# Gate and up stage: where the loads, sums and stores of the blocks without a partner stand

## The chip, the cores and the metric

The kernel runs on one core of a Trainium2 chip. The metric is the device time of one execution in microseconds (us). Five engines work side by side, each in its own order, and wait for one another through semaphores: TensorE (PE; its weight loads are listed as PEld), VectorE (DVE), ScalarE (ACT), GpSimd (POOL) and SyncE (SP). In this kernel SyncE and GpSimd do little but issue DMAs; a DMA whose buffer or data is not ready holds up the ones behind it in its queue.

## The reference

One input x of 2048 positions by 640 features goes through two branches, and a gate per position mixes them.

```python
def _A_ref(x, dft_seq_re, dft_seq_im, dft_hid_re, dft_hid_im):
    a = jnp.einsum("bsd,ed->bse", x, dft_hid_re)
    b = jnp.einsum("bsd,ed->bse", x, dft_hid_im)
    y = jnp.einsum("ts,bse->bte", dft_seq_re, a) - jnp.einsum("ts,bse->bte", dft_seq_im, b)
    return y

def _B_ref(x, w_gate, w_up, w_down):
    return (_gelu(x @ w_gate) * (x @ w_up)) @ w_down

x = A_x
g = _sigmoid((x * gate_w).sum(-1, keepdims=True))
a = _A_ref(x, A_dft_seq_re, A_dft_seq_im, A_dft_hid_re, A_dft_hid_im)
b = _B_ref(x, B_w_gate, B_w_up, B_w_down)
return g * a + (1 - g) * b
```

The hidden width of the second branch is 1728, that is 13 blocks of 128 and one of 64. All values are 32-bit floats.

## The kernel before

**Products.** Every operand of a product is split into a high part in the matrix format (written by ScalarE, helper `high`, L80) and a low part, the rest (written by VectorE, helper `low`, L83). `mm3` then issues three matmuls for one product, high by high, high by low and low by high (L99, L100, L101). On top of that the large products are done in the manner of Strassen: of a two by two product of blocks only seven block products are computed, from sums of the operands, so weights, inputs and hidden values are all needed as sums too. VectorE makes these sums.

**Stages.** The gate and up stage comes first and computes the hidden values, block after block of the hidden width. The down stage follows, then the two DFT products. Hidden values are stored to DRAM as they are made, with their sums (`hA`, `hT`, by `keep`, L390, on GpSimd's queue), and are read again in the down stage, which starts after some 300 us.

**Blocks.** Block 0 and the narrow block of 64 are computed before the loop; the loop at L1174 runs blocks f = 1 to 12. `pair_of(f)` gives a block's kind: 0 for blocks 1 and 2, then 1 for the odd blocks and 2 for the even ones from 3 on (an odd and the next even block share some products, `together` and `together_up`). `gate_up` (L487) is the work of one block on one half of the positions (tp = 0 and 1), in steps that the loop takes turns with: a matmul group, then what ScalarE or VectorE does with its bank. Three places matter here. In L537 VectorE adds bank X to `s5`; in L546 TensorE then adds the product of the u5 weights to the same bank X, so it has to wait until both halves' L537 have read; in L541 and L542 the other half of the block's result is summed and sent through gelu.

**Fills.** What VectorE and ScalarE must do for the next block (splits and sums of its weights, `make_w`; wa, wb, wq and ws are such weight tiles, ra, rb and rq their raw loads) stands in a list, `fills`, of pairs of a cost and a piece of work. `fill` (L1150) issues pieces between the steps, as many as are due: the costs done so far are held to 1.25 times the share of the block's matmul work that is issued. What is left in the list is issued at the block's end.

```python
while fills and not (some and not fills[0][0]) and state["done"] <= 1.25 * state["all"] * state["pe"] / state["pe_all"]:
    cost, do = fills.popleft()
```

**The blocks without a partner.** The hidden width has 14 blocks; the down stage pairs blocks 1 to 12 and is left with block 0 and the narrow block. Their hidden values (`h0`) and down weights (`wd0`, `wdr`) need sums of their own. `LEFT_AT` (L677) gives these to five blocks of the gate and up stage: to blocks 2 and 8 `sum_h0` (three loads, three sums, four stores to `hL`; tiles lf), to blocks 6 and 10 `sum_h0_narrow` (six loads, three sums, one store; tiles lg), to block 4 `sum_left` (five loads, six sums, two stores to `wsl`; tiles lw, lm, ld, ls). Each of these functions issues its loads at once, on SyncE's queue, and returns the sums as pieces for `fills`; a piece issues its stores behind its sums, on SyncE's queue as well. The loop calls the function at the block's start and puts the sums into the middle of `fills`, ahead of the second half of the next block's weight work. Only the down stage reads `hL` and `wsl`.

**Order and buffers.** TensorE, ScalarE, VectorE and GpSimd keep the written order here (`in_order`, L1173). SyncE's DMAs are not in that list: the recording layer lets one go ahead as soon as its tile has a buffer, so their order in the queue can differ from the written one. The tiles of 128 by 512 (`mtile`, L73: the lf, lg, lw tiles, the s tiles of `gate_up`, the xp and xv tiles of sums over positions, loaded for block 3's shared products) share 14 buffers; one that a store reads is free once the store has landed. SyncE's queue also carries the next blocks' weights (`load_w(f + 2)` in step 5 of a block, L1244; `load_up` and `sum_wd`, tiles wu, dr and da, at the start of an odd block) and the tiles xz of the gate's sum over features (L726, L730). GpSimd's queue carries `keep` and loads of sums over positions (xq and xu, L1145).

Of the kernel before, what the change touches and what calls it, by code (L numbers as in the profile page):

```python
# [23 lines left out]
FR = F - NF * P  # L24
# [11 lines left out]
def kernel(  # L36
# [27 lines left out]
    nc = tc.nc  # L64
# [5 lines left out]
    def slot(dt, shape, name):  # L70
        return pool.tile(shape, dt, tag="s4", name=name, bufs=46)

    def mtile(dt, name):  # L73
        return pool.tile([P, T], dt, tag="m", name=name, bufs=14)
# [30 lines left out]
    @contextmanager  # L105
    def in_order(*engines):

        traced = nc.cur_bb.bb.instructions
        mark = traced[-1]
        yield  # L110
        start = next(k for k in reversed(range(len(traced))) if traced[k] is mark) + 1
        dep = mybir.DependencyInfo(mybir.DependencyClass.NoSync, mybir.DependencyReason.DATA)
        prev = {}
        for ins in traced[start:]:
            if ins.engine in engines:
                if ins.engine in prev:
                    tc.add_manual_dep(ins, prev[ins.engine].name, dep, reason="in_order")
                prev[ins.engine] = ins
# [10 lines left out]
    wsl = dram.tile([P, 8, P], F32, tag="wsl", name="wsl")  # L129
    hL = [dram.tile([P, 4, T], F32, tag=f"hL{p}", name=f"hL{p}") for p in range(2)]  # L130
# [476 lines left out]
    def chunks(name):  # L607
        return mtile(F32, name).rearrange("p (b c) -> p b c", c=P)

    def sum_left():  # L610


        w, m, d = chunks("lw"), chunks("lm"), chunks("ld")
        nc.sync.dma_start(w, wd0[:, :4])
        for q in range(2):
            rows = slice(q * FR, (q + 1) * FR)
            nc.sync.dma_start(m[rows], wdr[:, :4])
            nc.sync.dma_start(d[rows], wd0[:FR, :4])
        a11, a21, a22 = w[:, 0:2], w[:, 2:4], m[:, 2:4]
        own = {}  # L620

        def first():
            s = own["s"] = chunks("ls")
            tt(s[:, 0:2], a21, a11, op=ALU.subtract)
            tt(a21[:FR], a21[:FR], a22[:FR], op=ALU.add)
            tt(m[:, 0:2], m[:, 0:2], a22, op=ALU.subtract)

        def second():
            s = own["s"]
            tt(a11, a11, a21, op=ALU.subtract)  # L630
            tt(d[:, 0:2], d[:, 0:2], d[:, 2:4], op=ALU.subtract)
            tt(s[:, 2:4], m[:, 0:2], d[:, 0:2], op=ALU.add)
            nc.sync.dma_start(wsl[:, 0:4], w)
            nc.sync.dma_start(wsl[:, 4:8], s)

        return [(100, first), (100, second)]

    def sum_h0(tp):


        f1, f2, b22 = (mtile(F32, f"lf{tp}{k}") for k in range(3))
        for v, k in ((f1, 0), (f2, 1), (b22, 3)):
            nc.sync.dma_start(v, h0[tp][:, k])

        def first():
            tt(f1, f2, f1, op=ALU.subtract)
            for k in (0, 2):
                rows = slice(FR if k else 0, P)
                nc.sync.dma_start(hL[tp][rows, k], f1[rows])
            tt(f2[:FR], f2[:FR], b22[:FR], op=ALU.subtract)  # L650
            nc.sync.dma_start(hL[tp][:, 3], f2)
            tt(b22[:FR], f1[:FR], b22[:FR], op=ALU.subtract)
            nc.sync.dma_start(hL[tp][:FR, 2], b22[:FR])

        return [(183, first)]

    def sum_h0_narrow(tp):


        d1, d2, b21, b22 = (mtile(F32, f"lg{tp}{k}") for k in range(4))  # L660
        for v, k in ((d1, 0), (d2, 1)):
            for q in range(2):
                nc.sync.dma_start(v[q * FR : (q + 1) * FR], h0[tp][:FR, k])
        for v, k in ((b21, 2), (b22, 3)):
            nc.sync.dma_start(v, h0[tp][:, k])

        def first():
            tt(d2, d2, d1, op=ALU.subtract)
            tt(b21, b21, b22, op=ALU.subtract)

        def second():
            tt(b21, b21, d2, op=ALU.add)
            nc.sync.dma_start(hL[tp][:, 1], b21)

        return [(122, first), (61, second)]

    LEFT_AT = {2: partial(sum_h0, 0), 4: sum_left, 6: partial(sum_h0_narrow, 0), 8: partial(sum_h0, 1), 10: partial(sum_h0_narrow, 1)}  # L677

# [464 lines left out]
    def load_across(f, n, to, kept, k):  # L1143
        v = slot(F32R, [P, 2, T], f"{n}{f}{k}")
        nc.gpsimd.dma_start(v.bitcast(F32), kept[k - 1])  # L1145
        to[f"T{k}"] = v[:, 0], v[:, 1]

    fills, state = deque(), {}
# [24 lines left out]
    with in_order(PE, ACT, DVE, POOL):  # L1173
        for f in range(1, NF):  # L1174
            kind = pair_of(f)
            if f == PAIRED:
                loadu()
                fills.extend([*t4, *u123[:3], *late_work, *u123[3:], *u4])
            fills.extend(todo)
            todo.clear()  # L1180
            if kind == 1:
                up, work = make_up(f, load_up(f))
                fills.extend(work)
            if kind == 1:
                lw, *w = sum_wd((f - PAIRED) // 2)
                lw[1]()
                fills.extend(w)
            if f == PAIRED - 1:
                loadp()
                fills.extend(t123)  # L1190
            if f == NF - 1:
                lw, *w = sum_wd(NK - 1)
                lw[1]()
                fills.extend(w)
            if f + 1 < NF:
                nxt, work = make_w(f + 1)
                if kind != 1 or f == PAIRED:
                    fills.extend(work)
            if kind == 1 and f > PAIRED:
                (_, first), z1, (_, second), z2 = load_z(2)  # L1200
                first()
                k = len(fills) // 2
                more = list(fills)
                fills.clear()
                fills.extend([*more[:k], z1, (0, second), *more[k:], z2, *work])
            elif f in ZE_AT:
                (_, first), z1 = load_z(1)
                first()
                fills.insert(5, z1)
            if f in LEFT_AT:  # L1210
                more = LEFT_AT[f]()
                k = len(fills) // 2
                rest = [fills.pop() for _ in range(len(fills) - k)]
                fills.extend([*more, *reversed(rest)])
            if f == NF - 1:
                load_k(0)
                fills.extend(split_pieces(0))
                gates(0)
                nc.scalar.activation(table, table, AF.Gelu_apprx_tanh)
            state.update(pe=0, done=0, all=sum(c for c, _ in fills), pe_all=2450 if not kind else 2994 if kind == 1 else 1768)  # L1220
            s5 = pair(F32, f"s5{f}")
            xs = {}
            work = [gate_up(f, W, Bs[tp], tp, s5[:, tp], s1t, xs, s4) for tp in range(2)]
            more = together(f, W, Tp, s1t, xs) if kind == 1 else iter(())
            more_up = together_up(f, W, up, s4) if kind == 1 else iter(())
            for _ in range(4):
                run(more)
            for step in range(8 if not kind else 7):
                for tp, w in enumerate(work):
                    run(w)  # L1230
                    if (step, tp) in ((0, 1), (1, 1)):
                        run(more)
                        if step == 0:
                            run(more)
                    if (2, 0) < (step, tp) < (6, 0):
                        run(more_up)
                if step < 2 and kind == 1 and f > PAIRED:
                    for k in ((1,), (2, 3))[step]:
                        load_across(f, "xu", Tu, keptu, k)
                if step == 4 and pair_of(f + 1) == 1 and f + 1 > PAIRED:  # L1240
                    for k in (1, 2, 3):
                        load_across(f + 1, "xq", Tp, keptp, k)
                if step == 5:
                    load_w(f + 2)  # L1244
                if f == NF - 1 and step > 4:
                    load_k(step - 4)
            for v in (more, more_up):
                next(v, None)
            while fills:
                fills.popleft()[1]()  # L1250
            W = nxt
# [80 lines left out]
    for i, (j, ri, b, sp) in enumerate(cseq):  # L1332
# [21 lines left out]
        if not b:  # L1354
# [17 lines left out]
            if lst:  # L1372
# [4 lines left out]
                for d in range(2):  # L1377
                    c = sv["c11", d]
# [83 lines left out]
    for i, (tp, b, p) in enumerate(useq[: 3 * ND]):  # L1462
# [22 lines left out]
        if not b:  # L1485
            for q in range(2):
                sv["c11", q] = copy(X[q], f"ys{n}{q}")
            for q in range(2):
                c = sv["c11", q]
# [76 lines left out]
    for ps, w, b, t in ((Z, "S4", 3, 1), (V, "A12", 2, 0)):  # L1566
        which = ends[2 - 2 * t : 4 - 2 * t]
        gated_high(which)
        for q in range(2):
# [3 lines left out]
            v = es[q][0] if t else sv["x", q]  # L1573
# [20 lines left out]
    for ps, cols in zip(parts_of, halves):  # L1594
# [3 lines left out]
        v = vs[1][:, cols]  # L1598
# [68 lines left out]
```

## Time and profile before

| | |
|---|---|
| runs of the kernel before | 1023.54, 1027.96, 1030.12 us (median 1027.96) |
| profiled execution | 1022.09 us, of which the span from first to last instruction is 1020.3 us |
| granted TensorE clock | 1.000 |
| DMA traffic | 269.15 MB, mean 264 GB/s |
| gate and up stage, blocks 2 to 10 | about 72 to 287 us |

A block of kind 0 lasts some 23 us in this profile, an odd block from 3 on 30 us, an even one 18 us. In a row of the timeline the columns are the start in us, the duration, engine, line and operation, what is written from what, and in brackets the engine's idle time just before and what ended it. A row of the waits gives the engine and tile that waited, what it waited for, and total, number and longest in us. Matmuls overlap: a row's duration reaches into the next matmul, so their rate is read from their starts.

### The profile page before, as it was taken

The page shows a single profiled execution, that of the slowest core. Times are in us where ns is not written, and L with a number is a line of the kernel's source. Part 1 is how long each engine was busy: PE and PEld are TensorE (multiplying, and loading weights), DVE is VectorE, ACT ScalarE, POOL GpSimd, SP SyncE. Part 2 cuts the span into 40 slices and gives each one's busy share as a digit, 9 for nine tenths or more (in the row PEclk, how much of TensorE's full clock was granted, in tenths as well). Part 3 has the DMA queues.
Part 4 walks back from the last instruction along what each step waited for, and adds up shares of the span by engine and source line. Part 5 has one row for each costly group of instructions (what it writes and reads, how often), then busy time and mean ns, then how long its engine had stood idle before and what let it go on. Part 6 is the DMA issues. An engine that isn't in the chain of part 4 may idle for free.

```text
span 1020.3 us, 13287 instructions
## 1 busy us (share of the span) xinstructions
PE 1015.7 (100%) x4483; PEld 839.3 (82%) x4483; DVE 824.0 (81%) x1163; ACT 486.0 (48%) x635; POOL 166.9 (16%) x295
## 2 busy tenths in 40 slices
PE   9999999999999999999999999999999999999998
PEld 7888878888888888888888888888888888888887
DVE  6977877787877979988898975897588859797796
ACT  5544534353635577466455343444344445455440
POOL 0122232323231200100011022102210200021112
PEclk9999999999999999999999999999999999999999
DMA  7456598979798999969766778658866877997856
GB/s 270 168 187 237 195 292 282 304 250 336 231 320 297 403 331 373 346 258 355 258 236 192 246 269 305 217 193 288 307 205 209 293 255 269 326 321 217 262 149 97
DMA packets 98084, 269.15 MB, mean 264 GB/s; under 512 B 12832, under 2 KB 28064, under 8 KB 98016
## 3 DMA queue, kind: packets, MB, share of 16 engines
q1 hardware_dynamic: 72096, 186.94, 53.1%
q0 software_dynamic: 25776, 81.30, 24.2%
q8 instruction: 35, 0.57, 0.2%
q14 instruction: 33, 0.27, 0.1%
q10 hardware_dynamic: 144, 0.07, 0.0%
HBM read 193.53 MB, written 70.80 MB: 259 GB/s over the span
## 4 chain that ended last, share of the span: by engine, by line
PE 88%; issue 8%; POOL 2%; DVE 1%; DMA 1%; POOLq 0%; DVEq 0%
PE pX L100 5%; PE pX L99 5%; PE pX L101 5%; PE pZ L100 4%; PE pZ L99 4%; PE pZ L101 4%; PE pL L99 3%; PE pL L100 3%; PE pL L101 3%; PE pY L99 1%; PE pQ L99 1%; PE pR L99 1%; PE pV L99 1%; PE pV L100 1%; PE pR L101 1%
## 5 line engine op out<-in xcount | busy, mean ns | idle before, releaser
L80 ACT ACTIVATE ch<-csa 128x1024 fp32r<-128x1024 f32 x32 | 34.0, 1063 | 89.4 <-DVE csa L777 70.6
L83 DVE TENSOR_TENSOR cl<-cra,ch 128x1024 fp32r<-128x1024 f32 x32 | 39.1, 1222 | 23.5 <-ACT ch L80 23.3
L80 ACT ACTIVATE ch<-cra 128x1024 fp32r<-128x1024 f32 x32 | 33.9, 1059 | 47.5 <-PE pL L100 15.3
L83 DVE TENSOR_TENSOR cl<-crb,ch 128x1024 fp32r<-128x1024 f32 x32 | 39.1, 1221 | 15.5 <-ACT ch L80 15.4
L101 PE MATMUL pL<-ch,xal 128*128 128x512 f32 x128 | 49.8, 389 | 0.0
L100 PE MATMUL pL<-cl,xah 128*128 128x512 f32 x128 | 49.8, 389 | 0.0
L99 PE MATMUL pL<-ch,xah 128*128 128x512 f32 x128 | 49.3, 389 | 0.0
L390 POOL DMA_DIRECT2D hA<-s x48 | 26.1, 544 | 126.7 <-DVE s L548 107.2
L80 ACT ACTIVATE ch<-crb 128x1024 fp32r<-128x1024 f32 x32 | 33.8, 1055 | 25.8 <-DVE cl L83 12.4
L83 DVE TENSOR_TENSOR cl<-csb,ch 128x1024 fp32r<-128x1024 f32 x32 | 39.1, 1223 | 4.3 <-ACT ch L80 2.3
L83 DVE TENSOR_TENSOR cl<-csa,ch 128x1024 fp32r<-128x1024 f32 x32 | 39.1, 1222 | 2.9 <-PE pR L100 1.7
L80 ACT ACTIVATE ch<-csb 128x1024 fp32r<-128x1024 f32 x32 | 34.0, 1062 | 12.5 <-PE pR L101 4.5
L83 DVE TENSOR_TENSOR kl<-kw,kh 128x1024 fp32r<-128x1024 f32 x26 | 31.7, 1220 | 6.5 <-ACT kh L80 6.5
L542 ACT ACTIVATE s<-s 128x512 f32<-128x512 f32 x24 | 15.2, 633 | 45.2 <-DVE s L541 45.2
L1328 POOL DMA_DIRECT2D uA<-c x8 | 4.3, 541 | 169.8 <-DVE c L1416 169.6
L914 POOL DMA_DIRECT2D out<-ks x12 | 6.5, 542 | 153.8 <-DVE ks L913 153.1
L390 POOL DMA_DIRECT2D hT<-s x48 | 26.0, 541 | 26.9 <-DVE s L565 9.3
L147 ACT ACTIVATE s<-pX 128x512 f32<-128x512 f32 x40 | 23.1, 596 | 14.8 <-PE pX L101 14.3
L80 ACT ACTIVATE kh<-kw 128x1024 fp32r<-128x1024 f32 x26 | 27.2, 1048 | 2.1 <-DMA kw<-wsd 2.1
L101 PEld LDWEIGHTS pL<-ch,xal 128*128 128x128 f32 x128 | 24.0, 188 | 5.0
L99 PEld LDWEIGHTS pL<-ch,xah 128*128 128x128 f32 x128 | 24.0, 188 | 5.0
L100 PEld LDWEIGHTS pL<-cl,xah 128*128 128x128 f32 x128 | 24.0, 188 | 5.0
(3612 smaller groups left out, 3467.9 us busy)
## 6 DMA issues: line engine op xcount, KB each, us to landing
cra<-in_ct SPq DMA_DIRECT2D x64, 512.0 KB, 4.0
crb<-in_ct SPq DMA_DIRECT2D x64, 512.0 KB, 5.2
hA<-s POOLq DMA_DIRECT2D x48, 256.0 KB, 4.5
hT<-s POOLq DMA_DIRECT2D x48, 256.0 KB, 5.7
kr<-hA SPq DMA_DIRECT2D x24, 512.0 KB, 7.3
kr<-hT SPq DMA_DIRECT2D x24, 512.0 KB, 7.5
ux<-uA SPq DMA_DIRECT2D x24, 512.0 KB, 6.1
ux<-uT SPq DMA_DIRECT2D x16, 512.0 KB, 5.8
```

The source lines that it names most:

```text
L80: nc.scalar.activation(hi, raw, AF.Copy)
L83: nc.vector.tensor_tensor(lo, raw, hi.bitcast(F32), op=ALU.subtract)
L99: nc.tensor.matmul(ps, lh, rh, start=first, stop=False, skip_group_check=True)
L100: nc.tensor.matmul(ps, lh, rl, start=False, stop=False, skip_group_check=True)
L101: nc.tensor.matmul(ps, ll, rh, start=False, stop=last, skip_group_check=True)
L147: nc.scalar.activation(m, src, AF.Copy)
L390: nc.gpsimd.dma_start(to[:, i], src)
L542: nc.scalar.activation(s2, s2, AF.Gelu_apprx_tanh)
L914: nc.gpsimd.dma_start(acc4[:, t] if tp and e == 4 else out[2 * tp + t, e], src)
L1328: nc.gpsimd.dma_start(to[:, i], src)
```

## The change

The five functions keep their loads and sums. Their stores are no longer issued behind the sums but gathered in a list, `left_out`, which the loop issues when the next block begins. The loop calls the function after step 3 of the block instead of at its start, and appends the sums to the end of `fills`, adding their costs to the block's total then.

```diff
         def second():
             ...
-            nc.sync.dma_start(wsl[:, 0:4], w)
-            nc.sync.dma_start(wsl[:, 4:8], s)
+            left_out.append((wsl[:, 0:4], w))
+            left_out.append((wsl[:, 4:8], s))
 ...
             for k in (0, 2):
                 rows = slice(FR if k else 0, P)
-                nc.sync.dma_start(hL[tp][rows, k], f1[rows])
+                left_out.append((hL[tp][rows, k], f1[rows]))
 ...
             tt(b21, b21, d2, op=ALU.add)
-            nc.sync.dma_start(hL[tp][:, 1], b21)
+            left_out.append((hL[tp][:, 1], b21))
 ...
+    left_out = []
 ...
             if f == PAIRED:
                 loadu()
                 fills.extend([*t4, *u123[:3], *late_work, *u123[3:], *u4])
+            for to, v in left_out:
+                nc.sync.dma_start(to, v)
+            left_out.clear()
             fills.extend(todo)
 ...
-            if f in LEFT_AT:
-                more = LEFT_AT[f]()
-                k = len(fills) // 2
-                rest = [fills.pop() for _ in range(len(fills) - k)]
-                fills.extend([*more, *reversed(rest)])
 ...
+                if step == 3 and f in LEFT_AT:
+                    left = LEFT_AT[f]()
+                    fills.extend(left)
+                    state["all"] += sum(c for c, _ in left)
                 if step == 5:
                     load_w(f + 2)
```

The two other stores of `sum_h0` are changed in the same way.

More of the change, by code (lines that the diff above doesn't have):

```diff
@@ L648, in first @@
                 rows = slice(FR if k else 0, P)
-                nc.sync.dma_start(hL[tp][rows, k], f1[rows])
+                left_out.append((hL[tp][rows, k], f1[rows]))
             tt(f2[:FR], f2[:FR], b22[:FR], op=ALU.subtract)
-            nc.sync.dma_start(hL[tp][:, 3], f2)
+            left_out.append((hL[tp][:, 3], f2))
             tt(b22[:FR], f1[:FR], b22[:FR], op=ALU.subtract)
-            nc.sync.dma_start(hL[tp][:FR, 2], b22[:FR])
+            left_out.append((hL[tp][:FR, 2], b22[:FR]))
         return [(183, first)]
```

## The prediction

> **What bounds the kernel now.** I read the page first, then the waits of TensorE, then the gate and up stage alone.
>
> ```profile
> span 1020.3 us, 13287 instructions
> PE 1015.7 (100%) x4483; PEld 839.3 (82%) x4483; DVE 824.0 (81%) x1163; ACT 486.0 (48%) x635; POOL 166.9 (16%) x295
> ...
> PE idle L1015 <- PEq L1655: 0.8, 1, 0.8
> PE pH5t L99 <- DMA xq<-xp: 0.3, 1, 0.3
> ```
>
> The last two rows are all the waits that TensorE has in the whole span: 0.8 us at the start and 0.3 us before one matmul of block 5. A busy share of 100% could still hide slow matmuls, so I look at their spacing, in the block where the change puts most instructions, and at the window around it.
>
> ```profile
> 125.00:143.00 18.00, 18.00 (x81) 14.93 (x80) 14.99 (x33) 9.43 (x15) 6.66 (x11) 1.00 0.81 228
> ...
> 141.45 0.39 PE L99 MATMUL pX<-x05h,wa 128*128 128x512 f32 x1
> ...
> 142.13 0.39 PE L99 MATMUL pX<-x15h,wa 128*128 128x512 f32 x1
> ...
> L100 PEld LDWEIGHTS pX<-x011l,wa 128*128 128x128 f32 x2 | 0.4, 188 | 0.1
> ```
>
> The first row is the table by stretches (stretch, length, busy time of TensorE, its weight loads, VectorE, ScalarE and GpSimd, then the granted clock, the DMA share and GB/s), the next two are from the timeline, the last groups weight loads by form. Three products lie between the two matmuls shown, so starts are 0.68 / 3 = 0.227 us apart, at a granted clock of 1.00. 4483 matmuls at 0.227 us are about 1016 us of the 1020.3 us span. So everything that is not a matmul following a matmul is worth about 4 us, 0.4%, and the change touches no matmul. That is the ceiling of any gain. What the change can do is turn VectorE's or SyncE's order into a new wait of TensorE; the working below asks how much slack each moved step has.
>
> The Trainium skill (Perfetto Trace Analysis, Identifying the Most-Contended Engine) speaks against this reading: it calls TensorE's matmul busy share a poor measure of headroom and prefers the share of weight loads, here 82%, by which some 18% of the span, an estimate of 184 us, would be open. In this trace it is not: each load takes 188 ns of a 227 ns spacing, 83%, so the loads' share is what back-to-back matmuls give.
>
> **The change part by part.** Work is neither added nor removed: the same 18 sums, 23 loads and 12 stores. The build keeps TensorE's order the same. VectorE's order changes in blocks 2, 4, 6, 8 and 10 alone: the sums go from ahead of the next block's weight sums (ws) to behind the last weight split (ws low), next to L537, which reads bank X for s5. TensorE waits for that read before it adds the u5 product to X. This is the tightest place, so I take it first, in block 4 with its six sums.
>
> ```profile
> 131.57 0.42 DVE L624 TENSOR_TENSOR ls<-lw 128x256 f32<-128x256 f32 x1
> ...
> 133.82 0.42 DVE L271 TENSOR_TENSOR ws5r<-wb,wa5r 128x256 f32<-128x256 f32 x1
> ...
> 137.14 0.29 DVE L83 TENSOR_TENSOR wd<-wb,wd 128x128 fp32r<-128x128 f32 x1 [1.57 <-ACT wd L80]
> 137.35 1.22 DVE L83 TENSOR_TENSOR ws5l<-ws5r,ws5h 128x1024 fp32r<-128x1024 f32 x1
> 138.49 1.28 DVE L537 TENSOR_TENSOR s<-s,pX 128x512 f32<-128x512 f32 x2
> ...
> 135.34 0.62 ACT L533 ACTIVATE s<-s 128x512 f32<-128x512 f32 x1
> 135.86 1.05 ACT L80 ACTIVATE ws5h<-ws5r 128x1024 fp32r<-128x1024 f32 x1
> 136.81 0.30 ACT L80 ACTIVATE wd<-wb 128x128 fp32r<-128x128 f32 x1
> ```
>
> The six sums take 133.82 - 131.57 = 2.25 us. Removing them there lets the weight sums run 2.25 us earlier, but VectorE then still waits for ScalarE's wd, as it does now for 1.57 us: ScalarE is what ends that wait. So the sums leave a place where 1.57 us of them was hidden and come to a place where they are not. Without any help from ScalarE, L537 starts at 138.49 + 2.25 = 140.74 and its two instructions end about 141.4 and 142.02; TensorE needs them at 141.45 and 142.13. That is just in time, with 0.05 and 0.1 us left. But the build also puts ws5h and wd ahead of the first gelu (L533): 135.86 - 135.34 = 0.52 us earlier, if ws5r is ready, which it is. So L537 starts near 140.2 and 0.6 us of slack remains, against 2.3 us now. No wait of TensorE; 0 us.
>
> In blocks 6, 8 and 10 there are three sums of 0.68 us, 2.05 us.
>
> ```profile
> 187.01 1.27 DVE L537 TENSOR_TENSOR s<-s,pX 128x512 f32<-128x512 f32 x2
> ...
> 190.64 0.39 PE L99 MATMUL pX<-x15h,wa 128*128 128x512 f32 x1
> ...
> 234.78 1.28 DVE L537 TENSOR_TENSOR s<-s,pX 128x512 f32<-128x512 f32 x2
> ...
> 238.35 0.39 PE L99 MATMUL pX<-x15h,wa 128*128 128x512 f32 x1
> ...
> 282.61 1.28 DVE L537 TENSOR_TENSOR s<-s,pX 128x512 f32<-128x512 f32 x2
> ...
> 286.25 0.39 PE L99 MATMUL pX<-x15h,wa 128*128 128x512 f32 x1
> ```
>
> The second L537 ends at 187.01 + 2.05 + 1.27 = 190.33, 238.11 and 285.94, before the needed 190.64, 238.35 and 286.25 by 0.3, 0.2 and 0.3 us even without ScalarE's 0.5 us, by 0.7 to 0.8 us with it. Again 0 us. What is late next is the chain behind L537 (L541, gelu, the product), by up to 1.7 us. In the next block VectorE stands before its z sum (L730) anyway, so it catches up:
>
> ```profile
> DVE xz L730 <- DMA hA<-s: 9.6, 3, 3.3
> ...
> DVE xz L730 <- DMA xz<-in_xz: 3.0, 1, 3.0
> ```
>
> These are VectorE's waits between 52 and 300 us (total, times, longest): four waits of some 3 us, one in each of the four blocks that follow.
>
> **The loads** are written in mid block but go out when SyncE reaches them and their buffers are free. In blocks 4 to 10 that is near the block's start as now, except the last one or two, whose buffers are freed by the previous block's products (L553). Block 8:
>
> ```profile
> 221.59 0.69 DVE L553 TENSOR_TENSOR s<-s,s 128x512 f32<-128x512 f32 x1
> ...
> DMA to landing us min/median/max: 2.8/3.5/5.7
> ```
>
> Issued at 222.3 and landed, by the slowest load of the lf tiles, at 228.0, for a sum that is now due after 234: 6 us to spare. 0 us.
>
> **The stores** wait on SyncE for the sums, and everything behind them in that queue waits too. SyncE's waits in the same stretch show what that is now:
>
> ```profile
> SPq L649 <- DVE lf L646: 30.6, 2, 19.3
> ```
>
> The longest, 19.3 us, is block 2's, and nothing behind it was due. With the change the loads of lf wait for buffers that the xp sums free, ahead of 78.97 in the row below; they land by 78.97 + 5.7 = 84.7, before their sums. The four loads of xv, for the sums of block 3, are split: two go ahead of the stores and two behind them. Behind these stand loads of wu3r, dr and da, issued some 3 us later than now, for a first read at 110.78 (its row is below). The build makes the third xv load wait until the second store has landed (they share a completion semaphore).
>
> ```profile
> 78.97 0.68 DVE L646 TENSOR_TENSOR lf<-lf,lf 128x512 f32<-128x512 f32 x1
> ...
> 89.05 0.68 DVE L537 TENSOR_TENSOR s<-s,pX 128x512 f32<-128x512 f32 x1
> ...
> 93.00 0.39 PE L99 MATMUL pX<-xT14h,wa2h 128*128 128x512 f32 x1
> ...
> 82.02 2.60 SPq L1110 DMA_DIRECT2D xv<-t  x4
> ...
> DMA to landing us min/median/max: 4.8/5.0/5.1
> ...
> DMA to landing us min/median/max: 2.2/3.4/5.7
> ```
>
> The lower row of landings (least, median, most) is that of the hL stores in this stage, the one above it that of the xv loads. The lf sums now stand between the two L537 of block 2: the second starts at 89.05 + 2.05 = 91.1 and ends at 91.8, for a TensorE need at 93.00; 0 us. The first sum ends near 89.7, the second store goes out near 90.2, lands at 93.6, and the xv load behind it lands at 93.6 + 5.0 = 98.6.
>
> ```profile
> 97.16 0.69 DVE L1115 TENSOR_TENSOR xv<-xv,xv 128x512 f32<-128x512 f32 x1
> 98.43 0.69 DVE L83 TENSOR_TENSOR xv<-xvt,xv 128x512 fp32r<-128x512 f32 x1 [0.57 <-ACT xv L80]
> 99.88 0.60 ACT L147 ACTIVATE s<-pH3t 128x512 f32<-128x512 f32 x1 [0.65 <-DVE xv L1118]
> 101.84 0.40 PE L99 MATMUL pH3t<-xp,wq3h 128*128 128x512 f32 x1
> ...
> 110.78 0.28 DVE L240 TENSOR_TENSOR wu3r<-wu3r 128x128 f32<-128x128 f32 x1
> ```
>
> L1115 needs that load: 1.4 us later than 97.16. 0.57 us of it goes into the idle time of the next row; the copy of pH3t, released by L1118, moves by 0.9 to 100.8 and ends at 101.4; TensorE needs it at 101.84. 0.4 us remains, 0 us of cost; the far bound is a store that lands in 5.7 instead of 3.4 us, which makes TensorE 1.9 us late. I take 0, since 3.4 is the median.
>
> GpSimd's order of DMAs is unchanged. The sum of all parts is 0 us, between -0.3 (the one wait for xq gone) and +4.2 (the far bound above and that of rival (c) together).
>
> **The rivals.** (a) Late sums stop TensorE. Place: bank X before the u5 product in blocks 4, 6, 8 and 10. Price: one us for each us beyond the slack of 0.6 to 0.8 us. To be slower by 1%, 10.3 us, the sums would have to end 10.3 / 4 + 0.7 = 3.3 us later than I place them in each block; with 1 us it costs 1.2 us. For it: the slack falls from 2.3 to 0.6 us. Against it: the loads have 6 us to spare. At the deciding 3.3 us: 1038 us. (b) The xv chain of block 3: +1.9 us, 1030. (c) The two stores of block 4 now go out at about 139.5 and 140.5, not where the sums stand above, but just ahead of the loads of xq that end the one DMA wait of TensorE:
>
> ```profile
> wsl<-lw SPq DMA_DIRECT2D x1, 256.0 KB, 2.7
> ...
> 141.61 1.22 POOL L1145 DMA_DIRECT2D xq<-xp  x2 [5.07 <-DMA wq5l<-wq5r]
> ```
>
> At the window's 228 GB/s, 512 KB are 2.3 us if none of it is done by 141.6: 1030. The Trainium skill (DMA: Bandwidth & Descriptors, Issuing engines are not separate DMA queues) says that transfers of SyncE and GpSimd share the same DMA engines and interleave; no row here shows these two together. (d) The change does not do what it says: in blocks 6 and 10 the build puts the one store behind the wa and wu loads of the next block, and most loads go out when they did; then nothing moves, 1028. (e) Weights ready 2 us earlier make matmuls start earlier: no wait of TensorE on them exists now, at most 4 us, 1024; and by the skill's measure of headroom more.
>
> **How the numbers follow.** The profiled execution took 1022.1 us, 1.8 around its span; the runs shown are 1023.5, 1028.0 and 1030.1. The forecast of 0 us gives 1028.0 for the median. Nothing below 1% (10 us) can be told from no change here. Chances: no wait 0.73 with (d) 0.05 in it, (b) 0.08, (c) 0.08, (a) under 1% 0.03, over 1% 0.06, (e) 0.02. The range goes from just under the fastest execution, 1021, to the slowest run plus (b) and (c), 1030.1 + 4.2 = 1034. Faster by over 1%: 0.02, needing more than TensorE's gaps hold. Slower by over 1%: 0.07. Within: 0.91.
>
> **What would show it.** Right: the waits of TensorE stay at two rows; the sums stand between ws low and L537; L537 starts near 140.2 in block 4 with no wait of pX behind it. Wrong: a row "PE pX <- DVE s L537" (a), "PE pH3t <- ACT s" near 102 (b), or the wait on xq grown from 0.3 us (c); or a matmul spacing other than 0.227 us, which nothing above foresees.

## The result, and the profile after

| | before | after |
|---|---|---|
| median of 22 runs | 1027.13 us | 1033.14 us |
| lowest to highest | 1023.54 to 1032.18 | 1029.53 to 1039.23 |
| profiled execution (its span) | 1022.1 us (1020.3) | 1029.7 us (1027.9) |

The ratio is 1.0060, with a 95% interval of 1.0045 to 1.0076: the change costs 6.0 us. That is inside the forecast range, and below the 1% under which the prediction thought that nothing could be told from no change. With 22 executions of each kernel it can be told: the interval leaves out 1, and the forecast was 0.

The page of the changed kernel begins like this, and the second fence holds all its waits of TensorE (total, times, longest, in us). Lines further down in the program have other numbers than in the kernel before: its L730 is L732 here, its L1145 is L1147.

```profile
span 1027.9 us, 13294 instructions
...
PE 1016.9 (99%) x4483; PEld 838.8 (82%) x4483; DVE 823.4 (80%) x1163; ACT 485.8 (47%) x635; POOL 167.5 (16%) x295
```

```profile
PE pH5t L99 <- DMA xq<-xp: 2.4, 1, 2.4
PE pH11t L99 <- DMA xq<-xp: 1.2, 1, 1.2
PE pH7t L99 <- DMA xq<-xp: 1.2, 1, 1.2
PE pH7t L99 <- DVE s L440: 0.9, 1, 0.9
PE idle L1017 <- PEq L1659: 0.8, 1, 0.8
PE pH9t L99 <- DVE s L440: 0.4, 1, 0.4
PE pH11t L99 <- DVE s L440: 0.2, 1, 0.2
PE pm L100 <- DVE x012l L83: 0.2, 1, 0.2
```

TensorE's busy time has hardly moved (1015.7 to 1016.9 us). Its waits have grown from 1.1 to 7.3 us, and these 6.2 us are most of the 7.6 us between the two spans. The busy share goes from 100% to 99%: it hints at the loss, and only the list of waits shows where it is. Nearly all of it is in the odd blocks, behind two things, the loads of xq and VectorE's L440.

No wait stands at bank X. The timeline of the changed kernel shows block 4's sums where the prediction put them:

```profile
137.09 0.29 DVE L83 TENSOR_TENSOR wd<-wb,wd 128x128 fp32r<-128x128 f32 x1 [3.31 <-ACT wd L80]
...
138.43 0.42 DVE L624 TENSOR_TENSOR ls<-lw 128x256 f32<-128x256 f32 x1
...
140.69 1.28 DVE L537 TENSOR_TENSOR s<-s,pX 128x512 f32<-128x512 f32 x2
...
141.91 0.39 PE L99 MATMUL pX<-x05h,wa 128*128 128x512 f32 x1
...
142.59 0.39 PE L99 MATMUL pX<-x15h,wa 128*128 128x512 f32 x1
```

TensorE reaches this place 0.46 us later than before (141.91 against 141.45), so L537 at 140.69 is the forecast 140.2. The second of the two ends at 140.69 + 1.28 = 141.97, 0.6 us ahead of the matmul at 142.59. Three products in 0.68 us are 0.227 us each, as before. VectorE waits 3.31 us for ScalarE's wd where the sums used to stand.

What did move is the DMAs. First the two queues of the changed kernel around the end of block 4 (SPq is SyncE's queue; the first number is the time of issue):

```profile
126.55 0.48 SPq L618 DMA_DIRECT2D ld<-in_wd  x1
...
128.36 0.59 SPq L218 DMA_DIRECT2D wb<-in_wf  x1
128.99 0.44 SPq L599 DMA_DIRECT2D da<-in_wd  x1
129.48 0.97 SPq L218 DMA_DIRECT2D wb<-in_wf  x1
...
131.13 0.90 POOL L95 DMA_DIRECT2D wa5l<-wa5r  x1 [0.28 <-issue]
...
138.63 0.57 POOL L1147 DMA_DIRECT2D xq<-xp  x1 [2.91 <-DVE ws5l L83]
...
140.00 0.33 SPq L1182 DMA_DIRECT2D wsl<-lw  x1
140.80 0.33 SPq L1182 DMA_DIRECT2D wsl<-ls  x1
...
141.47 1.22 POOL L1147 DMA_DIRECT2D xq<-xp  x2 [2.27 <-DVE s L537]
```

And the same place in the kernel before (its last two xq loads stand in the prediction, at 141.61):

```profile
130.67 0.90 POOL L95 DMA_DIRECT2D wa5l<-wa5r  x1 [0.28 <-issue]
...
133.13 0.33 SPq L633 DMA_DIRECT2D wsl<-lw  x1
...
134.31 0.46 SPq L218 DMA_DIRECT2D wb<-in_wf  x1
...
135.98 0.57 POOL L1145 DMA_DIRECT2D xq<-xp  x1 [0.72 <-DVE wb L290]
```

Between 126.55 and 130.45 us SyncE now issues six loads of 128 KB: the last three loads of the sums and, queued behind them, three small loads of weights, wb, da and wb. SyncE's own waits name what held them:

```profile
SPq L618 <- DVE s L553: 5.4, 1, 5.4
```

Right after these six GpSimd issues wa5l, a transfer that adds the raw tile of the wa weights to their negated high part and so makes the low part (L95; the expectations call it the copy of wa_l). wq5l is the next of this kind. The view of DMA issues gives its size and its time to landing, in the changed kernel:

```profile
wa5l<-wa5r POOLq DMA_DIRECT2D x1, 512.0 KB, 6.8
wa7l<-wa7r POOLq DMA_DIRECT2D x1, 512.0 KB, 8.3
...
wa9l<-wa9r POOLq DMA_DIRECT2D x1, 512.0 KB, 5.5
...
wa11l<-wa11r POOLq DMA_DIRECT2D x1, 512.0 KB, 8.0
```

and the fastest and the slowest of the same four in the kernel before:

```profile
wa5l<-wa5r POOLq DMA_DIRECT2D x1, 512.0 KB, 4.5
...
wa9l<-wa9r POOLq DMA_DIRECT2D x1, 512.0 KB, 4.8
```

The first xq load goes into the buffer of the raw weights that this transfer reads, so it is issued 0.7 us after that has landed: 131.13 + 6.8 + 0.7 = 138.63, against 135.98. The name in its bracket, ws5l, is only what the profile put the wait down to; the program makes it wait for the landing of wa5l. So the copy, slowed by its neighbours, pushes the first xq load toward the other two, and there the two stores now stand as well, 1.5 and 0.7 us ahead of them. Those other two follow wq5l in the same way: they are issued some 0.4 us after it has landed (134.85 + 6.2 + 0.4 = 141.47). In blocks 7 and 11 this second copy is slower too, 6.7 and 7.1 us against 5.6 and 6.0, so there the last two xq loads are late as well as the first.

That gives two suspects, the late loads and the late stores, and a third wait to explain, L440. The next odd block shows where that one comes from:

```profile
207.72 0.83 DVE L732 CUSTOM_DVE_ANT_0 xz<-xz,gwb 128x640 f32<-128x640 f32 x1 [5.56 <-DMA xz<-in_xz]
...
208.47 0.68 DVE L440 TENSOR_TENSOR s<-s,pH7t 128x512 f32<-128x512 f32 x1
```

VectorE stands for 5.56 us before the gate's sum (3.0 to 3.3 us before), and L440, which TensorE needs, is written behind it. What ends this wait is the landing of xz. In blocks 5, 7, 9 and 11 the first xz now lands after 11.8, 12.3, 10.3 and 11.2 us (8.9 to 9.2 before), and the sum starts 0.1 to 0.2 us later each time, also where the bracket names another transfer.

### The profile page after: what moved, and what is told of

The parts are those of the page before. It is cut to its first block, busy times and chain, and to the rows that moved or that the text cites. A ratio compares the mean times of both kernels' runs of the same rounds, so it can differ in the third digit from the quotient of the medians.

```text
span 1027.9 us, 13294 instructions
## 1 busy us (share of the span) xinstructions
PE 1016.9 (99%) x4483; PEld 838.8 (82%) x4483; DVE 823.4 (80%) x1163; ACT 485.8 (47%) x635; POOL 167.5 (16%) x295
## 4 chain that ended last, share of the span: by engine, by line
PE 85%; issue 5%; DMA 5%; DVE 3%; POOL 1%; ACT 0%; SPq 0%; POOLq 0%; DVEq 0%
PE pX L101 5%; PE pX L100 5%; PE pX L99 5%; PE pZ L101 3%; PE pZ L99 3%; PE pZ L100 3%; PE pL L101 3%; PE pL L99 3%; PE pL L100 3%; PE pV L101 2%; PE pV L99 2%; PE pV L100 2%; PE pY L101 1%; PE pR L101 1%; PE pQ L101 1%
## 5 line engine op out<-in xcount | busy, mean ns | idle before, releaser
L147 ACT ACTIVATE s<-pX 128x512 f32<-128x512 f32 x40 | 23.2, 595 | 14.8 <-PE pX L101 14.5
```

The lines of the kernel that those rows point to most:

```text
L147: nc.scalar.activation(m, src, AF.Copy)
```

## The experiments

All twelve were timed against the kernel before, with 7 to 12 executions each (the kernel before: 23 to 35). In the first three columns stands what differs.

| | loads of the sums | sums | stores | ratio, 95% interval |
|---|---|---|---|---|
| after | mid block | end | SyncE, next block | 1.0060, 1.0045 to 1.0076 |
| 1 | block's start | end | SyncE, next block | 0.9975, 0.9954 to 0.9995 |
| 2 | mid block | end | left out | 1.0015, 0.9998 to 1.0031 |
| 3 | block's start | end | left out | 0.9976, 0.9960 to 0.9993 |
| 4 | mid block | end | SyncE, behind the sums | 1.0075, 1.0044 to 1.0105 |
| 5 | mid block, 15 buffers | end | SyncE, next block | 0.9980, 0.9960 to 1.0001 |
| 6 | before, 15 buffers | middle | as before | 0.9992, 0.9968 to 1.0016 |
| 7 | block's start | middle | left out | 0.9967, 0.9944 to 0.9990 |
| 8 | block's start, 15 buffers | end | SyncE, next block | 0.9972, 0.9948 to 0.9996 |
| 9 | mid block | end | GpSimd, next block | 1.0049, 1.0028 to 1.0070 |
| 10 | block's start | middle | GpSimd, next block | 1.0031, 1.0013 to 1.0050 |
| 11 | mid block | end | as 9, block 2's on SyncE | 0.9999, 0.9981 to 1.0017 |
| 12 | block's start | middle | as 10, block 2's on SyncE | 0.9961, 0.9942 to 0.9979 |

### Loads or stores: runs 1 to 4

Run 1 moves the call of the five functions back to the block's start (and with it the moment at which the sums' costs enter the block's total), and nothing else.

```diff
-                if step == 3 and f in LEFT_AT:
-                    left = LEFT_AT[f]()
-                    fills.extend(left)
-                    state["all"] += sum(c for c, _ in left)
 ...
+            if f in LEFT_AT:
+                fills.extend(LEFT_AT[f]())
             if f == NF - 1:
```

> As the changed kernel, but the loads of the sums stand at the block's start again, as before; sums and stores stay late. Theory L (late loads): in the changed kernel the last loads wait in SyncE's queue for buffers that L553 frees, and they and the small loads behind them (wb, da) share the DMA engines with GpSimd's copy of wa_l, which then lands after 6.8, 8.3, 5.5 and 8.0 us instead of 4.5 to 4.8; xq reuses the buffers of the raw weights, goes out later by as much, and TensorE waits for it. By it wa_l lands after 4.5 to 5.5 us here in blocks 4, 6, 8 and 10, the waits of TensorE on xq fall from 4.8 us in all to under 0.7, and the ratio to before is 1.000 (0.998 to 1.002). Rival S (late stores): the stores that go out at 140 us share the engines with the loads of xq; then the wait on xq in block 5 stays at about 2.4 us, those in blocks 7 and 11 at about 1.2, and the ratio stays at 1.005 or more. A mixture shows 2.4 us in block 5 and nothing in 7 and 11, 1.002 to 1.003.

Measured: 1024.47 us against 1026.39. No wait on xq is left, and wa_l lands after 4.5, 5.7, 5.2 and 5.0 us. So the loads' place is what makes the copy late, and with it undone the loss is gone, though the stores still go out at 139.78 and 140.58 us, right ahead of the xq loads. That it comes out below 1 was not expected; runs 7 and 12 ask why. L440 still makes TensorE wait, 1.8 us in block 9, where xz lands after 11.7 us, and 0.7 in block 5.

Run 2 keeps the loads in mid block and leaves out the stores of blocks 4, 6, 8 and 10; GpSimd fills `wsl` and `hL` from `h0` earlier, while it is idle, so the down stage reads other values from them.

```diff
             for to, v in left_out:
-                nc.sync.dma_start(to, v)
+                if f == 3:
+                    nc.sync.dma_start(to, v)
             left_out.clear()
```

> As the changed kernel, but the stores of the sums of blocks 4, 6, 8 and 10 are left out (wsl and hL get other contents of the same size from GpSimd's queue some 20 us earlier, where it is idle). The loads stay in mid block. Theory L: wa_l still lands after 6.8 to 8.3 us in blocks 4, 6 and 10, TensorE still waits for xq over 3 us in all, ratio to before 1.004 to 1.007. Rival S: the waits on xq fall to about 0.3 us in all, dr lands after 8 to 9 us in the odd blocks as before instead of 10 to 11, and the ratio is 1.000 to 1.002. A mixture: the wait in block 5 (2.4 us) falls under 1 us, those in blocks 7 and 11 stay at 1.2, 1.003.

Measured: 1.0015. wa_l lands as late as in the changed kernel (6.9, 8.2, 6.5 and 7.6 us), TensorE still waits for xq, 1.3 us in block 7 and 3.1 in block 11, but not in block 5. The ratio is that of the rival, the landings are those of theory L, and so is the sum of the waits on xq (4.4 us, over 3 expected); that block 5's wait alone is gone is what was named for a mixture. Neither theory holds alone.

> The two edits before together: the loads at the block's start, and the late stores left out (wsl and hL get other contents earlier). Both theories: no wait of TensorE on xq above 0.5 us, ratio to before 1.000 (0.998 to 1.002). If TensorE still waits here, neither the loads nor the stores are the cause, but the late sums themselves or the small loads of wb and da that are no longer held behind a store.

Run 3 makes both edits. Measured: 0.9976, with 0.6 us of waits on xq (0.5 at most was expected); TensorE also waits 1.5 us for L440 and 0.5 for L476, and wa_l lands after 6.0 and 5.5 us in blocks 4 and 6 (4.5 and 5.7 in run 1). Beside run 1 (0.9975) the stores cost nothing when the loads are early; beside run 2, in the changed kernel's order, they cost 1.0060 - 1.0015 = 0.45%. So in these four kernels the stores hurt only where xq is late, and the late loads alone cost 1.0015 - 0.9976 = 0.39%. The loss then adds up from run 1 on: -0.25 (run 1) + 0.39 + 0.45 = 0.6%.

> As the changed kernel, but each store is written right behind its sum, not in the next block. SyncE's order of transfers comes out the same as in the changed kernel. Both theories: the same waits as in the changed kernel (xq 2.4, 1.2 and 1.2 us, L440 0.9, 0.4 and 0.2, each within 0.5) and a ratio to before of 1.005 to 1.007; writing the stores in the next block is then a part of the change without effect. A rival by which the deferral itself costs gives 1.000 to 1.002.

Run 4 writes each store behind its sum again. Measured: 1.0075, within the intervals as slow as the changed kernel, and the stores of block 4 go out at 139.98 and 140.78 us (140.00 and 140.80): the program line that defers the stores has no effect seen here, since the sums themselves are late. But the waits did not repeat one by one. TensorE waited 0.2 us for xq in block 5 and 2.2 for L440 in the same block. One profiled execution tells the place of a loss of this size only roughly; the ratios and the landings repeat better.

### What holds the loads: runs 5, 6 and 8

```diff
-        return pool.tile([P, T], dt, tag="m", name=name, bufs=14)
+        return pool.tile([P, T], dt, tag="m", name=name, bufs=15)
```

> The changed kernel with 15 instead of 14 buffers for the tiles of 128x512; no line moves. What this asks: is it the buffer that holds the late loads (a tile takes the buffer of the one 14 tiles back, in the changed kernel a product of the block before that L553 frees), or the place in the code? With one more buffer each load's buffer was freed earlier: in block 4 by DMAs of the xv stage, in block 8 by DMAs, and in blocks 6 and 10 only the last load still waits for L553. Theory L with the buffer as the holder: wa_l of blocks 4 and 8 lands after 4.5 to 5.5 us as in the first experiment (6.8 and 5.5 in the changed kernel), that of 6 and 10 in between (5 to 7, from 8), the wait on xq in block 5 falls from 2.4 us to under 0.5, and the ratio to before is 0.997 to 1.002. If the place in the code holds them, nothing moves: 1.004 to 1.008.

> The control to the run before: the kernel before with 15 buffers. Its loads go out at the block's start in any case, so a buffer more changes nothing there: the same waits as before (under 0.7 us on xq) and a ratio of 0.998 to 1.002. If it were 0.995 or less, the additional buffer would help by itself and the run before would prove nothing on the loads.

The changed kernel with one buffer more gives 0.9980, the kernel before with the same buffer 0.9992. These are the one wait of TensorE in this stage and the landings in the changed kernel with 15 buffers:

```profile
PE pH9t L99 <- DVE s L440: 1.3, 1, 1.3
...
```

```profile
wa5l<-wa5r POOLq DMA_DIRECT2D x1, 512.0 KB, 4.5
wa7l<-wa7r POOLq DMA_DIRECT2D x1, 512.0 KB, 6.3
...
wa9l<-wa9r POOLq DMA_DIRECT2D x1, 512.0 KB, 4.8
...
wa11l<-wa11r POOLq DMA_DIRECT2D x1, 512.0 KB, 6.4
```

Blocks 4 and 8, where no load waits for L553 any more, are back at 4.5 and 4.8 us; blocks 6 and 10, where one still does, lie in between, as expected. No wait on xq is left. The place in the code costs nothing by itself, then: it costs because the tile at that place is given a buffer that a product of the block before has just used. The control's profile had 3.6 us of waits on xq, mostly in block 11, where wq11l took 7.8 us (6.0 in the profile of the kernel before); the kernel before is close to this edge too.

> The first experiment's kernel (loads at the block's start, late sums and stores) with 15 buffers, as the candidate that could be best. Theory: the buffers do not bind there, so the ratio is that of the first experiment, 0.9975 (0.995 to 1.000). It would be lower, to 0.995, if the waits of TensorE on L440 (1.8 and 0.7 us in the first experiment) come from buffers of this ring that free late.

Run 8 gave 0.9972: as run 1, within the intervals. L440 still waits 1.6 us, so that wait doesn't come from these buffers.

### Where the gain comes from: runs 7, 10 and 12

> The kernel before (loads at the block's start, sums in the middle of VectorE's work) without the stores of the sums of blocks 4, 6, 8 and 10 (wsl and hL get other contents of the same size from GpSimd's queue earlier). It asks where the gain of the first experiment (0.9975) comes from. In the kernel before, the small loads of wb and da stand in SyncE's queue behind stores that wait for the sums and go out at 134 us in block 4, beside the copy of wq_l; without the stores they go out near 122. Theory W (the small loads, freed, leave the copies of wq_l and the first xq alone): 0.996 to 0.999, and wq5l lands after about 5 us instead of 6.8. Rival V (the gain is VectorE's: the late sums let the weight sums go first): then nothing is gained here, 0.999 to 1.003.

Run 7 has the order of the kernel before but no stores in four blocks. Measured: 0.9967, with 0.5 us of waits on xq and none on L440; wq_l landed after 5.4, 4.1, 4.1 and 6.1 us (6.8, 5.6, 5.2, 6.0 before). The small loads went out at 127.5 us in block 4, not near 122, as the loads ahead of them were late. The gain needs no late sums. What runs 1, 3, 5, 7 and 8 have in common is that wb and da are not held behind a store that waits for the sums, and start to go out 4 us or more ahead of the copies. They share a second thing, which no run tells from the first: no store goes out just ahead of the copy of wq_l either, as the two of block 4 do in the kernel before (133.13 and 133.93 us, the copy at 134.39).

> A candidate that computes everything: loads at the block's start and sums in the middle of VectorE's work as in the kernel before, the stores on GpSimd's queue in the next block, so that nothing holds the small loads of wb and da on SyncE. Theory W: wq_l lands after 5.4 us or less in blocks 6 and 8 (5.6 and 5.2 before) and after less than 6.5 in blocks 4 and 10, TensorE waits for xq under 0.7 us and not for L440, ratio 0.997 (0.995 to 0.999). Rival V (the sums' place makes the gain): 0.999 to 1.002. A third way: GpSimd's queue now has two to four more transfers of some 0.55 us ahead of hT, and if one of them delays xu, TensorE waits there and the ratio is above 1.002.

Run 10 was to be that with everything computed: loads and sums as before, the stores on GpSimd's queue in the next block. Measured: 1.0031. The landings were as theory W had them (wq_l after 5.1, 4.4, 4.1 and 4.8 us), the ratio missed by the place of one wait, 5.7 us of `pH3t` on ScalarE's L147 in block 3. Run 9 has the same wait and shows it below: block 2's stores went out late on that queue, and the xv loads of block 3 take the buffers that these stores free. Run 12 leaves block 2's stores on SyncE:

```diff
             for to, v in left_out:
-                nc.sync.dma_start(to, v)
+                (nc.sync if f == 3 else nc.gpsimd).dma_start(to, v)
             left_out.clear()
```

> The tenth run once more, with block 2's stores left on SyncE's queue (on GpSimd's they made a wait of 5.7 us in block 3). Loads at the block's start, sums in mid block, the later stores on GpSimd's queue. Theory W (what is gained comes from the small loads of wb and da that no store holds any more): no wait in block 3, none on xq above 0.5 us, none on L440, ratio 0.997 (0.995 to 0.999), as in the seventh run (0.9967) but with everything computed. Rival V (the sums' place makes the gain): 0.999 to 1.002.

Measured: 1023.29 us against 1027.36, ratio 0.9961. It has the lowest ratio of the kernels here that compute everything (runs 1 and 8 lie within its interval), and its 12 executions lie within 2.3 us (1022.33 to 1024.59), those of the kernel before, beside it, within 9.5. These are all its waits of TensorE, and two of its landings:

```profile
PE idle L1017 <- PEq L1660: 0.8, 1, 0.8
PE pH9u L99 <- DMA xu<-xv: 0.4, 1, 0.4
PE pm L1048 <- ACT x011h L80: 0.3, 1, 0.3
```

```profile
wq5l<-wq5r POOLq DMA_DIRECT2D x1, 448.0 KB, 4.9
wq7l<-wq7r POOLq DMA_DIRECT2D x1, 448.0 KB, 4.1
```

### The stores beside xq: runs 9 and 11

> The changed kernel, but the stores go out on GpSimd's queue, behind the hA transfers of the odd block, so about 147 us instead of 140 in block 5: behind the loads of xq, not ahead of them. Nothing is left out. The loads stay late: wa_l lands after 6 to 8.5 us in blocks 4, 6 and 10 as in the changed kernel. Theory (late loads make the xq loads late, and the stores beside them turn that into a wait in block 5): the wait in block 5 falls from 2.4 us to under 0.7, those in blocks 7 and 11 stay over 1 us each, and the ratio to before is 1.001 to 1.004, as without the stores (1.0015). Rival (the stores' share in the second experiment came from their buffers, which were freed earlier there, not from their transfers): the buffers are freed later here than in the changed kernel, so the ratio stays at 1.005 or more.

Run 9 is the changed kernel with all stores on GpSimd's queue. Measured: 1.0049; as in run 10, a new wait hid what was asked:

```profile
96.68 6.21 SPq L1112 DMA_DIRECT2D xv<-t  x2
96.99 2.28 POOL L1182 DMA_DIRECT2D hL<-lf  x4
...
103.12 0.69 DVE L1116 TENSOR_TENSOR xvt<-xv,xv 128x512 f32<-128x512 f32 x1 [6.47 <-DMA hL<-lf]
...
107.22 0.79 PE L99 MATMUL pH3t<-xp,wq3h 128*128 128x512 f32 x1 [5.10 <-ACT s L147]
```

> The ninth run once more, with block 2's stores left on SyncE's queue: on GpSimd's they held the xv loads of block 3, and TensorE waited 5.1 us there, which hid what was asked. Now only the stores of blocks 4, 6, 8 and 10 go out behind the xq loads. Theory (late loads make xq late, the stores beside xq turn that into the wait of block 5): wa_l still lands after 6 to 8.5 us in blocks 4, 6 and 10; no wait of 5 us in block 3; the wait on xq in block 5 under 0.7 us (2.4 in the changed kernel), those in blocks 7 and 11 together 1.5 to 4.5; ratio to before 1.000 to 1.003, as without the stores (1.0015). Rival (buffers, not transfers): 1.005 or more.

Run 11 leaves block 2's stores where they were. Measured: 0.9999. The loads are as late as in the changed kernel (wa_l after 6.9, 8.4, 5.9 and 8.2 us), TensorE waits for xq 1.0 us in block 7 and 1.6 in block 11, and not in block 5. There the stores go out at 147.80, behind xq, and the landing of the two xq loads that end the block's DMA chain differs like this, first in the kernel before, then in the changed kernel, then in run 11:

```profile
xq<-xp POOLq DMA_DIRECT2D x2, 512.0 KB, 6.5
```

```profile
xq<-xp POOLq DMA_DIRECT2D x2, 512.0 KB, 8.2
```

```profile
xq<-xp POOLq DMA_DIRECT2D x2, 512.0 KB, 4.8
```

The rival, that the buffers of the stores and not their transfers cost the time, expected 1.005 or more and falls. By the Trainium skill (DMA: Bandwidth & Descriptors, Issuing engines are not separate DMA queues) transfers of different issuers interleave on the same DMA engines; the prediction had no row for stores of SyncE beside loads of GpSimd, and here it is: 8.2 us against 4.8 for a load of 512 KB, which agrees. The 3.4 us between them are not a price of the stores in general: in run 1, with the stores 0.7 us ahead of these loads but the first xq load issued early (136.05), they land after 6.7 us, about as in the kernel before, and TensorE does not wait.

## Why the prediction was right, and where it was not

- **Bound, spacing and ceiling.** Right for the profile: 0.227 us per product in both kernels, and the loss is gaps between matmuls. The ceiling was read off one execution of 1022.1 us, among the fastest of the kernel before. Its median lies 5 us higher, and run 12 took 4.1 us off that median.
- **The sums at bank X, rival (a).** Right in place and slack; no such wait in any of the runs.
- **The xv chain, rival (b).** No wait in the changed kernel. The chain was the right one to fear: runs 9 and 10, in which block 2's stores went out later still, wait exactly there, 5.1 and 5.7 us.
- **The loads.** Here the prediction failed, by the step "6 us to spare. 0 us". The placing was nearly right ("the last one or two"): in block 4 the last three of five loads were held, in blocks 6 and 10 the last two, in block 8 the last, by a wait for L553. But they were priced against the sums that read them alone. They, and the small loads that are now queued behind them and no longer behind a store, run beside GpSimd's copy of wa_l, which takes 5.5 to 8.3 us in place of 4.5 to 4.8, and the first xq load follows from its landing. By runs 2 and 3 this step is worth 0.39%, some 4 us, where the sum had 0. "GpSimd's order of DMAs is unchanged" was true of the order, and was taken for the times.
- **The stores, rival (c).** The mechanism was right and the price close: issued at 140.00 and 140.80 us (forecast 139.5 and 140.5), and block 5's wait on xq grew by 2.42 - 0.35 = 2.07 us of the 2.3 allowed. It had a chance of 0.08, and 0 us in the sum. Run 11 gives its worth: with the stores of four blocks moved away, 1.0060 becomes 0.9999. That the price came out close is partly luck: it was worked out from the stores alone. But by runs 1 and 3 the stores cost nothing with early loads. Rival (c) was one half of a pair; the other half was the loads.
- **The catching up before xz.** Wrong in blocks 7, 9 and 11: the next block's wait before xz was no reserve, since xz itself landed later (10.2 us in the median of the stage, 8.7 before), and L440 behind it made TensorE wait 1.5 us in the profiled execution. What slowed xz was not tried apart.

Four things stay open. The last loads of the sums and the small loads of wb and da were not tried apart, so how much of the copy's delay belongs to each is not known. Where the gain of runs 7 and 12 comes from is open between two things: the small loads let go earlier, or the stores no longer just ahead of the copy of wq_l. Whether the sums' late place costs by itself is not settled either: a wait on L440 shows in eight of the nine profiles with late sums and, with 0.3 us, in one of the five with sums in the middle, but the ratios of runs 12 and 1 overlap. And that the wider spread of the kernel before comes from waits on xq in some of its executions is argued from run 6's profile, not shown.

## What to carry to other kernels

A load's place in the code is a place in a ring of buffers too: before moving it, find out whose buffer it will be given and when that is freed, and what stands behind it in its queue. A transfer has to be priced not only against its own reader but against every transfer that it newly runs beside, and against what waits for those; here the late stores cost nothing alone, and 0.45% once late loads had pushed xq toward them. And the same queue can hold a gain: moving a store that waits for late data, and holds loads behind it, out of the way was worth 0.4%, whether by the loads let go or by the store that no longer stands next to a copy.

## What was not expected of the hardware

A wait of TensorE costs more than its length. The table by stretches of run 9, around the wait of 5.1 us (the figure behind the counts is the granted clock), and of run 1, behind a wait of 1.84 us that ends at 254.70:

```profile
102.00:106.00 4.00, 0.12 (x1) 0.00 (x0) 2.27 (x4) 1.60 (x3) 0.51 (x1) 1.00 0.21 77
106.00:107.00 1.00, 0.00 (x0) 0.00 (x0) 0.96 (x2) 0.43 (x1) 0.60 (x2) 0.78 0.40 164
107.00:113.00 6.00, 5.78 (x14) 4.53 (x15) 4.96 (x8) 2.67 (x5) 2.11 (x4) 0.50 0.40 158
113.00:114.00 1.00, 1.00 (x5) 0.82 (x4) 0.99 (x2) 0.00 (x0) 0.06 (x1) 0.81 0.69 266
```

```profile
255.00:256.00 1.00, 1.00 (x5) 0.77 (x4) 0.97 (x4) 0.34 (x1) 0.00 (x0) 0.78 0.86 336
256.00:259.00 3.00, 3.00 (x9) 2.32 (x8) 2.86 (x7) 1.98 (x4) 0.91 (x2) 0.50 0.15 57
```

1.00 less the granted clock, times the stretch, sums to 0.22 + 1.50 = 1.7 us in run 1. That is time lost on top of the wait: 1.84 us of waiting cost 3.5. In run 9 the sum is 0.22 + 3.00 + 0.19 = 3.4 us, but the clock fell while TensorE still stood (its wait ends at 107.22), so only about 3 us of it come on top. Waits of 2.20 and 2.27 us in run 4, of 2.69 in run 6 and of 3.09 in run 2 did as in run 1; waits of 1.53 to 1.75 us in runs 3, 4, 8 and 11 did not, nor did the 2.42 us in the changed kernel's profile, whose clock is 1.00 on both sides. The Trainium skill (TensorE: Matmul & The Clock Gate, HAM oscillation — how this bites in real kernels) allows gaps up to about 3.4 us; in these runs a gap of 1.84 us was enough, so the measurement decides: such a gap may cost it, and does not always. Over the 22 timed executions of the changed kernel the granted clock averages 0.9978, which is about 2.2 us of the span; in the executions of the kernel before beside the experiments it was 0.8 to 1.5 us, in runs 11 and 12 it was 0.1 to 0.2. By these averages about 1 us of the 6 is this echo of the waits, an estimate, since each execution's clock is known to 0.001.
